# Taking maxima over partitions on TensorE and VectorE instead of GpSimd in a talking-heads attention and gated feed-forward kernel

## The chip, the cores and the metric

The kernel runs on one core of a Trainium2 chip. The metric is the device time of one execution in microseconds (us); the lower the better. Engines are named as the profile names them: PE is TensorE's matrix multiplication and PEld its loading of stationary operands, DVE is VectorE, ACT is ScalarE, POOL is GpSimd, SP is SyncE, which here only issues DMA transfers. An engine's name with a q behind it (POOLq, SPq) is its instruction queue.

## The reference

Attention for 4 batches, 12 heads, 448 tokens and 64 columns per head, in which the heads are mixed before and after the softmax, and then a gated feed-forward layer over the 768 joined columns:

```python
scores = scale * np.matmul(q, k.transpose(0, 1, 3, 2))
scores = np.einsum('bhij,hg->bgij', scores, w_pre)
scores = scores - np.max(scores, axis=-1, keepdims=True)
attn = np.exp(scores)
attn = attn / (np.sum(attn, axis=-1, keepdims=True) + 1e-09)
attn = np.einsum('bhij,hg->bgij', attn, w_post)
x = np.matmul(attn, v)            # then rearranged to (4*448, 768)
...
xn = x / rms * rms_g
g = xn @ w_gate
silu = g * (1.0 / (1.0 + np.exp(-g)))
val = xn @ w_val
return (silu * val @ w_out).astype(np.float32)
```

## The kernel before

The kernel has two parts. Part A, some 540 us, is the attention; part B is the feed-forward layer, matrix products in which three passes over split operands stand in for one of high precision. The change lies in part A.

Part A cuts the work of a batch into 4 chunks of query rows (of 12, 11, 11 and 11 groups of 10 rows). One group of one chunk is a *step*; there are 180 steps, 45 to a batch. In a step the function `premix` multiplies the scores of all heads by the first mixing matrix (tile `sp`, L216), `rowmax` takes row maxima on DVE (`nm`, L221), `expo` takes the exponential and its sum on ACT (`e`, L227), and `norm` puts the reciprocal of the sum (`rp`, L236) into the second mixing matrix on POOL (`wn`, L238). Two steps later `postmix` multiplies by `wn` (`pm`, L246), and three steps later `evac_ah` on ACT and `evac_al` on DVE split the result into two halves of 16 bits (`ah`, L258 and `al`, L263). The scores of the next chunks (`qk`, L195 and L196, evacuated to `st` at L209 and sent to their places by DMA, `r<-st`, L212) and the products with V (`av`, L273 and L274) are spread over the steps.

The order is written by hand: the loop over `t` in `part_a` runs the jobs of the step, and then `premix`, `norm`, `av_mm`, `postmix`, `qk_mm` and the evacuations, each engine taking its instructions in the order in which they are written. A job is a function with the step at which it runs (or the first and the last) and what it costs POOL; `run_jobs` runs those that are due.

The tiles `qk` come from a PSUM pool of two buffers (`ps_q`, tag `qk`), used in turn as they come free.

V is split into two 16-bit halves, for which each head is scaled by its largest magnitude. For one batch `max_v` takes, head by head on DVE, the maximum along each partition's row (`vm`, L155), `top_v` the maximum of these over all 128 partitions on POOL (`va`, L159, the instruction PARTITION_ALL_REDUCE), `scale_v` the scales from it (L163 to L175, DVE), and `round_v` (ACT, L178) and `split_v` (POOL, L183 and L184) do the split:

```python
vam[b] = p2.tile([128, H], F32, name=f"va{b}", tag="va")
nc.gpsimd.partition_all_reduce(vam[b], vmx.pop(b), 128, bass_isa.ReduceOp.max)
```

This happens in the third step of the second chunk for the first batch (step 11), and in the third step of a batch for the others (steps 47, 92 and 137, counted from 0). Before the steps, `setup` uses the same instruction once, for the column maxima of the second mixing matrix (`mpost`, L91).

Of the kernel before, what the change touches and what calls it, by code (L numbers as in the profile page):

```python
# [8 lines left out]
F32 = mybir.dt.float32  # L9
# [4 lines left out]
ALU = mybir.AluOpType  # L14
# [20 lines left out]
@with_exitstack  # L35
def attention_moe(ctx: ExitStack, tc, q, k, v, wpre, wpost, mask, ident, wgv, wo, rms_g, out):
    nc = tc.nc
# [39 lines left out]
    we = pro.tile([120, H], F32, name="we", tag="ksm2")  # L77
    wp = pro.tile([128, H], F32, name="wp", tag="ksm3")
    inv = pro.tile([128, H], F32, name="inv", tag="ksm4")

    def load_consts():
        nc.gpsimd.memset(wp, 0.0)
        nc.sync.dma_start(msk.rearrange("p a r -> p (a r)"), mask)
        nc.sync.dma_start(we, wpre)
        nc.sync.dma_start(wp[:120], wpost)

    def setup():
        nc.vector.tensor_scalar(we, we, D ** -0.5, None, ALU.mult)
        mt, mb = (msk[:, i].unsqueeze(1).to_broadcast([120, H, R]) for i in range(2))
        nc.vector.tensor_tensor(wk_pre, we.unsqueeze(2).to_broadcast([120, H, R]), mt, ALU.mult)  # L90
        nc.gpsimd.partition_all_reduce(mpost, wp, 128, bass_isa.ReduceOp.absmax)  # L91
        nc.vector.tensor_scalar(mpost, mpost, 1e-30, None, ALU.max)
        nc.vector.reciprocal(inv, mpost)
        nc.vector.tensor_tensor(wp, wp, inv, ALU.mult)
        nc.vector.tensor_tensor(wk, wp[:120].unsqueeze(2).to_broadcast([120, H, R]), mb, ALU.mult)


    kt, kraw, qhh, qll, qraw, vt, vraw, vmx, vam, vsc = ({} for _ in range(10))

# [50 lines left out]
    def max_v(b, part):  # L150
# [4 lines left out]
        nc.vector.tensor_reduce(vmx[b][:JP, h], vraw[b][:, h], AX.X, ALU.max, apply_absolute_value=True)  # L155

    def top_v(b):
        vam[b] = p2.tile([128, H], F32, name=f"va{b}", tag="va")
        nc.gpsimd.partition_all_reduce(vam[b], vmx.pop(b), 128, bass_isa.ReduceOp.max)  # L159

    def scale_v(b):
        am = vam.pop(b)
        nc.vector.tensor_scalar(am, am, 1e-30, None, ALU.max)  # L163
        sc = p2.tile([128, H], F32, name=f"vs{b}", tag="vs")
# [223 lines left out]
    def job(lo, hi, cost, f, *a):  # L388
        jobs.append([lo, hi, cost, f, a])

    pool_ = nc.gpsimd
    for n in range(NCHUNK):
# [13 lines left out]
        if c == 3 and b + 1 < B:  # L406
            for p in range(6):
                job(first[n] - 2 + p, 0, 0, load_v, b + 1, p)
            for h in range(H):
                t = first[n] + 3 + (14 * h) // 15  # L410
                job(t, t, 0, max_v, b + 1, h)
            job(first[n + 1] + 2, first[n + 1] + 2, 0.6, top_v, b + 1)
            job(first[n + 1] + 4, first[n + 1] + 4, 0, scale_v, b + 1)
        if n == 0:
# [4 lines left out]
            for h in range(H):  # L419
                t = 2 + (3 * h) // 4  # L420
                job(t, t, 0, max_v, 0, h)
            job(11, 11, 0.6, top_v, 0)
            job(12, 12, 0, scale_v, 0)
        if n == 4:
# [5 lines left out]
        if c == 0:  # L430
            for h in range(H):
                lo = av_step[n - 1, h] + 1 if n else 13
                job(lo, av_step[n, h] - 2, 1.1, round_v, b, h)
# [432 lines left out]
def layout(inputs):  # L866
# [14 lines left out]
    def cols(w, kt):  # L881
# [11 lines left out]
        "wpre": np.tile(inputs["w_pre"], (R, 1)),  # L893
        "wpost": np.repeat(inputs["w_post"], R, axis=0),
        "mask": np.concatenate([np.repeat(eye_r, H, axis=0), np.tile(eye_r, (H, 1))], axis=1),
        "ident": np.eye(JP, dtype=np.float32),
# [22 lines left out]
```

## Time and profile before

| | |
|---|---|
| median of 3 runs | 1097.96 us (1097.61 to 1099.19) |
| the profiled execution's own time | 1095.26 us |
| its span, first to last instruction | 1093.5 us |
| PE busy | 1012.9 us, 93% of the span |
| PEld, DVE, ACT, POOL busy | 854.0, 640.5, 495.2, 463.9 us |
| granted TensorE clock, mean over the span | 0.973 of full speed |
| DMA | 144.28 MB, mean 132 GB/s |
| chain that ended last | PE 65%, DMA 12%, DVE 10%, issue 7%, POOL 3% |

The busy time of an engine is the time in which it had an instruction in work; register, branch, semaphore and DMA-issuing instructions are left out of it. A number behind `x` is a count. In square brackets at the end of a timeline's row stands how long the engine was idle before that row and what ended the idle time; "issue" is time in which it waited for nothing that the profile shows. The granted clock is a share of full speed: 1.00 is 2.4 GHz, and 0.50 would be 1.2 GHz. Matmuls of 32-bit numbers count twice in the profile (`x8` for the four of `postmix`).

### The profile page before, as it was taken

How to read it: one execution, taken by the hardware profiler on the slowest of the kernel's cores; microseconds unless marked ns; L12 is line 12 of the kernel's file. 1: busy time of each engine (PE TensorE's matmuls, PEld its weight loads, DVE VectorE, ACT ScalarE, POOL GpSimd, SP SyncE). 2: the span in 40 equal slices, each digit the busy share in tenths (PEclk: the TensorE clock that was granted, in tenths of full speed). 3: DMA queues.
4: the chain of work that ended last, by engine and by line, in shares of the span. 5: the costliest groups of instructions: out<-in, count | busy, mean ns of one | idle time of the engine just before them, and what ended most of it. 6: DMA issues, size and time to landing. Idle time of an engine off the chain costs nothing.

```text
span 1093.5 us, 18212 instructions
## 1 busy us (share of the span) xinstructions
PE 1012.9 (93%) x6352; PEld 854.0 (78%) x6352; DVE 640.5 (59%) x1271; ACT 495.2 (45%) x1094; POOL 463.9 (42%) x576
## 2 busy tenths in 40 slices
PE   5859996999699996999998999999999998999998
PEld 2547774777477774877777999999999996999997
DVE  5536664776557664757759555555599996811100
ACT  4648874788578875877941111111111113422100
POOL 1345733676157643662544544444455553200000
PEclk9979997999989998999998999999999999999999
DMA  8636873668645775554442222222233436542100
GB/s 218 167 92 148 190 197 101 187 186 211 168 108 145 194 196 159 140 149 119 135 152 63 100 87 88 92 92 92 83 102 132 141 111 193 173 148 88 59 34 34
DMA packets 85969, 144.28 MB, mean 132 GB/s; under 512 B 21909, under 2 KB 76789, under 8 KB 85877
## 3 DMA queue, kind: packets, MB, share of 16 engines
q1 hardware_dynamic: 79541, 131.88, 41.3%
q0 software_dynamic: 6336, 11.22, 4.5%
q8 instruction: 51, 0.84, 0.3%
q14 instruction: 41, 0.34, 0.1%
HBM read 81.53 MB, written 22.83 MB: 95 GB/s over the span
## 4 chain that ended last, share of the span: by engine, by line
PE 65%; DMA 12%; DVE 10%; issue 7%; POOL 3%; ACT 2%; SPq 1%; POOLq 0%; DVEq 0%; ACTq 0%
PE pm L246 11%; PE sp L216 9%; DMA r<-st 7%; PE po L648 5%; PE po L649 5%; PE po L647 5%; PE pv L649 3%; PE qk L195 3%; PE pv L647 3%; PE pv L648 3%; PE pg L647 3%; PE pg L649 3%; PE pg L648 3%; PE qk L196 3%; PE av L273 2%
## 5 line engine op out<-in xcount | busy, mean ns | idle before, releaser
L246 PE MATMUL pm<-wn,e 120*112 120x120 f32 x1440 | 190.3, 276 | 45.6 <-POOL wn L238 45.1
L246 PEld LDWEIGHTS pm<-wn,e 120*112 120x112 f32 x1440 | 166.4, 181 | 61.6 <-POOL wn L238 52.0
L216 PE MATMUL sp<-r,wk_pre 120*120 120x448 f32 x360 | 170.9, 557 | 6.0 <-DMA qr<-in_q 5.7
L221 DVE TENSOR_REDUCE nm<-sp 120x1 f32<-120x448 f32 x180 | 111.7, 620 | 105.3 <-PE sp L216 103.6
L227 ACT ACTIVATE e<-sp,nm 120x448 f32<-120x448 f32 x180 | 113.7, 632 | 57.6 <-DVE nm L221 55.9
L238 POOL TENSOR_SCALAR wn<-wk,rp 120x120 f32<-120x120 f32 x180 | 65.9, 366 | 165.5 <-DVE rp L236 92.6
L263 DVE SCALAR_TENSOR_TENSOR al<-pm,ah 112x480 f16<-112x480 f32 x180 | 116.8, 649 | 11.4 <-ACT ah L258 11.2
L258 ACT ACTIVATE ah<-pm 112x480 f16<-112x480 f32 x180 | 101.9, 566 | 36.8 <-PE pm L246 36.0
L209 ACT ACTIVATE st<-qk 110x448 f32<-110x448 f32 (+1 forms) x186 | 100.3, 543 | 36.9 <-DMA r<-st 26.2
L579 ACT ACTIVATE wh<-wc 128x768 fp32r<-128x768 f32 x26 | 22.0, 847 | 193.7 <-DVE wc L555 193.7
L274 PEld LDWEIGHTS <-v 112*128 112x128 f16 x768 | 75.0, 98 | 43.1 <-issue 43.1
L195 PE MATMUL qk<-k,qh 128*110 128x448 f32 (+1 forms) x192 | 88.2, 459 | 15.7 <-ACT st L209 8.4
L647 PE MATMUL pv<-x,wh 128*128 128x448 f32 x264 | 97.5, 369 | 2.3 <-ACT wh L579 2.3
L273 PEld LDWEIGHTS <-v 112*128 112x128 f16 x768 | 74.5, 98 | 31.2 <-issue 29.6
L649 PE MATMUL pv<-x,wl 128*128 128x448 f32 x264 | 97.5, 369 | 1.1 <-POOL wl L580 1.1
L648 PE MATMUL pv<-x,wh 128*128 128x448 f32 x264 | 97.1, 368 | 0.0
L647 PE MATMUL pg<-x,wh 128*128 128x448 f32 x264 | 96.9, 367 | 0.0
L580 POOL TENSOR_TENSOR wl<-wc,wh 128x768 fp32r<-128x768 f32 x26 | 48.9, 1880 | 112.2 <-ACT wh L579 112.2
L649 PE MATMUL pg<-x,wl 128*128 128x448 f32 x264 | 96.3, 365 | 0.0
L648 PE MATMUL pg<-x,wh 128*128 128x448 f32 x264 | 96.2, 364 | 0.0
L273 PE MATMUL av<-ah,v 112*128 112x110 f16 (+1 forms) x768 | 94.6, 214 | 0.0
L274 PE MATMUL av<-al,v 112*128 112x110 f16 (+1 forms) x768 | 93.9, 213 | 0.1
(146 smaller groups left out, 2122.7 us busy)
## 6 DMA issues: line engine op xcount, KB each, us to landing
r<-st SPq DMA_DIRECT2D x144, 192.5 KB
wraw<-in_wgv SPq DMA_DIRECT2D x20, 768.0 KB
hd<-sg SPq DMA_DIRECT2D x48, 224.0 KB
hraw<-hd SPq DMA_DIRECT2D x48, 224.0 KB
r<-st SPq DMA_DIRECT2D x48, 210.0 KB
wraw<-in_wo SPq DMA_DIRECT2D x12, 768.0 KB
qr<-in_q SPq DMA_DIRECT2D x36, 220.0 KB
qh<-in_q POOLq DMA_DIRECT2D x33, 220.0 KB, 4.4
```

What stands on the lines that cost most here:

```text
L195: nc.tensor.matmul(ps[:m, :S], qhh[n][:, h], kk, start=True, stop=False)
L216: nc.tensor.matmul(ps[:120, :S], wk_pre.rearrange("p h r -> p (h r)"), rt[n][:120, g], start=True, stop=True)
L221: nc.vector.tensor_reduce(t, sps[n, g][:120, :S], AX.X, ALU.max, negate=True)
L227: nc.scalar.activation(e, sps.pop((n, g))[:120, :S], AF.Exp, bias=nmx.pop((n, g)), accum_out=s)
L246: nc.tensor.matmul(o, e[:, c * JP : (c + 1) * JP], w, start=True, stop=True)
L258: nc.scalar.activation(av[n, g][0], src, AF.Copy, scale=float(2.0 ** A_EXP))
L263: nc.vector.scalar_tensor_tensor(l_, src, float(2.0 ** A_EXP), h_, ALU.mult, ALU.subtract)
L273: nc.tensor.matmul(o, w[:, c_], ah[n][:, c_, h, :m], start=(c_ == 0), stop=False)
L274: nc.tensor.matmul(o, w[:, c_], al[n][:, c_, h, :m], start=False, stop=(c_ == JC - 1))
L647: nc.tensor.matmul(ps, a, xh[:, kk], start=(i == 0), stop=False)
L648: nc.tensor.matmul(ps, a, xl_[:, kk], start=False, stop=False)
L649: nc.tensor.matmul(ps, a2, xh[:, kk], start=False, stop=(i == n - 1))
```

## The change

`partition_all_reduce` is gone. In `setup` a DMA brings the second mixing matrix, transposed by the host, to all 128 partitions (`wa`, 128 x 144 numbers), and DVE takes the maxima along the row. For V, `top_v` becomes four jobs in four consecutive steps, one in each: `turn_v` transposes the 112 x 12 maxima by a matmul with the identity into a `ps_q` buffer (tile `vt`); `top_v` takes the maximum along the row on DVE and puts it on the diagonal of a 12 x 12 tile (`vo`, `vd`); `spread_v` multiplies a tile of ones by this diagonal, which puts the 12 maxima on all 128 partitions, in a second `ps_q` buffer (tile `va`); `scale_v` goes on from there. `max_v` runs up to one step earlier, `round_v` may start a step or two later.

```diff
     def load_consts():
-        nc.gpsimd.memset(wp, 0.0)
         nc.sync.dma_start(msk.rearrange("p a r -> p (a r)"), mask)
         nc.sync.dma_start(we, wpre)
-        nc.sync.dma_start(wp[:120], wpost)
+        nc.sync.dma_start(wp, wpost)
+        nc.sync.dma_start(wa, wpall)
...
-        nc.gpsimd.partition_all_reduce(mpost, wp, 128, bass_isa.ReduceOp.absmax)
+        nc.vector.tensor_reduce(mpost, wa.rearrange("p (g h) -> p g h", h=H), AX.X, ALU.max, apply_absolute_value=True)
...
+    def turn_v(b):
+
+        vps[b] = ps_q.tile([128, 512], F32, name="vt", tag="qk")
+        nc.tensor.matmul(vps[b][:H, :JP], vmx.pop(b)[:JP], eye, start=True, stop=True)
+
     def top_v(b):
-        vam[b] = p2.tile([128, H], F32, name=f"va{b}", tag="va")
-        nc.gpsimd.partition_all_reduce(vam[b], vmx.pop(b), 128, bass_isa.ReduceOp.max)
+        m = p2.tile([H, 1], F32, name=f"vo{b}", tag="vo")
+        nc.vector.tensor_reduce(m, vps.pop(b)[:H, :JP], AX.X, ALU.max)
+        vam[b] = p2.tile([H, H], F32, name=f"vd{b}", tag="vd")
+        nc.vector.tensor_scalar(vam[b], eye[:H, :H], m, None, ALU.mult)
+
+    def spread_v(b):
+        vps[b] = ps_q.tile([128, 512], F32, name="va", tag="qk")
+        nc.tensor.matmul(vps[b][:, :H], ones[:H], vam.pop(b), start=True, stop=True)
 
     def scale_v(b):
-        am = vam.pop(b)
-        nc.vector.tensor_scalar(am, am, 1e-30, None, ALU.max)
+        am = p2.tile([128, H], F32, name=f"va{b}", tag="va")
+        nc.vector.tensor_scalar(am, vps.pop(b)[:, :H], 1e-30, None, ALU.max)
...
-                t = first[n] + 3 + (14 * h) // 15
+                t = first[n] + 3 + (13 * h) // 15
                 job(t, t, 0, max_v, b + 1, h)
-            job(first[n + 1] + 2, first[n + 1] + 2, 0.6, top_v, b + 1)
-            job(first[n + 1] + 4, first[n + 1] + 4, 0, scale_v, b + 1)
+            for i, f in enumerate((turn_v, top_v, spread_v, scale_v)):
+                job(first[n + 1] + 2 + i, first[n + 1] + 2 + i, 0, f, b + 1)
...
-            job(11, 11, 0.6, top_v, 0)
-            job(12, 12, 0, scale_v, 0)
+            for i, f in enumerate((turn_v, top_v, spread_v, scale_v)):
+                job(10 + i, 10 + i, 0, f, 0)
...
-                lo = av_step[n - 1, h] + 1 if n else 13
+                lo = max(av_step[n - 1, h] + 1, first[n] + 6) if n else 14
                 job(lo, av_step[n, h] - 2, 1.1, round_v, b, h)
```

How this moves instructions, at three places. Line numbers of the changed kernel are 11 higher from the middle of the file on (L238 becomes L249, L246 becomes L257, L195 becomes L206). First POOL in the first batch, around step 11, before the change. Rows named ISA without a tile set up POOL's code; the trace calls them MODIFY_POOL_CONFIG. `L159 ISA va` is the PARTITION_ALL_REDUCE.

```order
L139 TENSOR_TENSOR ql_292<-qr_293,qh_291 128x440
L159 ISA
L159 ISA va_596<-vm_297 128x12
L238 ISA
L238 TENSOR_SCALAR wn<-wk,rp 120x120
L132 DMA qh_631<-in_q 128x440
L238 TENSOR_SCALAR wn<-wk,rp 120x120 x2
L183 TENSOR_SCALAR v_0_690<-vr_266 112x4x64
L184 TENSOR_TENSOR v_0_690<-vr_266,v_0_690 112x4x64
```

The same place after it:

```order
L132 DMA qh_631<-in_q 128x440
L249 TENSOR_SCALAR wn<-wk,rp 120x120 x2
L132 DMA qh_631<-in_q 128x440
L249 TENSOR_SCALAR wn<-wk,rp 120x120
L194 TENSOR_SCALAR v_0_728<-vr_267 112x4x64
L195 TENSOR_TENSOR v_0_728<-vr_267,v_0_728 112x4x64
...
L194 TENSOR_SCALAR v_3_737<-vr_267 112x4x64
L195 TENSOR_TENSOR v_3_737<-vr_267,v_3_737 112x4x64
L249 TENSOR_SCALAR wn<-wk,rp 120x120
```

The three ISA rows are gone, here and at the other three places, and no row of that name is left on POOL but those at the program's start and end. In this batch alone, four heads are split in one step between two `wn`, where before there were two and two; in the other batches POOL's order is otherwise the same.

Second PE at the same place in the changed kernel, with the semaphores that each row waits for; `vt` is `turn_v`, `va` is `spread_v`.

```order
L160 MATMUL vt<-eye,vm_298 12x112 [waits DMAHW5_49,DVE_49,Activation_49]
L227 MATMUL sp<-r_162,wk_pre 120x448
L257 MATMUL pm<-wn,e 112x120 [waits DVE_49,PE_49,Pool_49]
L257 MATMUL pm<-wn,e 112x120 x3
L206 MATMUL qk<-k_1_125,qh_292 110x448 [waits DVE_49]
L207 MATMUL qk<-k_1_125,ql_293 110x448
L227 MATMUL sp<-r_162,wk_pre 120x448 [waits Activation_49]
...
L170 MATMUL va<-vd_601,ones 128x12 [waits DVE_49,Activation_49]
...
L206 MATMUL qk<-k_2_129,qh_292 110x448 [waits DVE_49]
```

The matmul `vt` stands ahead of a step's `sp`, and the `qk` of that step, which before waited for an evacuation on ACT, now waits for DVE: it gets the buffer of `vt`, and waits until `top_v` has read it. The `qk` two places further on waits in the same way for `scale_v` to read `va`. The other three batches have the same pattern.

Third DVE in the changed kernel, from the end of the step of `turn_v`:

```order
L232 TENSOR_REDUCE nm<-sp 120x1
L274 SCALAR_TENSOR_TENSOR al_354<-pm,ah_353 112x48x10
L164 TENSOR_REDUCE vo_599<-vt 12x1
L166 TENSOR_SCALAR vd_601<-eye,vo_599 12x12
L245 TENSOR_SCALAR t<-s 120x1
```

The read of `vt` (L164) stands behind `nm` and `al` of the step in which PE made `vt`, and ahead of everything of the next step.

## Rows read from the trace of the kernel before

**Rows 1.** Waits over the whole span: waiting row, releaser, us in total, times, longest.

```profile
POOL wn L238 <- issue: 29.7, 4, 7.8
PE pm L246 <- POOL wn L238: 45.1, 9, 11.4
PE qk L195 <- ACT st L209: 8.4, 6, 2.2
```

**Rows 2.** Timeline of POOL, 154 to 182 us: start, duration, instruction, idle before.

```profile
158.59 0.36 POOL L238 TENSOR_SCALAR wn<-wk,rp 120x120 f32<-120x120 f32 x1 [1.53 <-DVE rp L236]
164.90 0.43 POOL L159 PARTITION_ALL_REDUCE va<-vm  x1 [5.95 <-DVE nm L221]
...
173.76 0.70 POOL L238 TENSOR_SCALAR wn<-wk,rp 120x120 f32<-120x120 f32 x2 [7.81 <-issue]
```

**Rows 3.** Groups of instructions, shapes apart: busy us, mean ns | idle before.

```profile
L159 POOL PARTITION_ALL_REDUCE va<-vm x4 | 1.7, 430 | 23.6 <-DVE nm L221 11.8 <-DVE rp L236 5.9 <-issue 5.9
L316 PE MATMUL pss<-ones,sum 128*112 128x1 f32 x32 | 3.4, 228 | 0.0
L184 POOL TENSOR_TENSOR v<-vr,v 112x256 f16<-112x256 f32 x48 | 34.0, 709 | 4.0
L183 POOL TENSOR_SCALAR v<-vr 112x256 f16<-112x256 f32 x48 | 22.0, 458 | 0.0
```

**Rows 4.** Timeline of PE, 162.5 to 186 us, second batch.

```profile
162.89 0.92 PE L216 MATMUL sp<-r,wk_pre 120*120 120x448 f32 x2
174.16 1.94 PE L246 MATMUL pm<-wn,e 120*112 120x120 f32 x8 [9.96 <-POOL wn L238]
...
180.76 0.92 PE L216 MATMUL sp<-r,wk_pre 120*120 120x448 f32 x2
...
183.19 0.92 PE L216 MATMUL sp<-r,wk_pre 120*120 120x448 f32 x2
```

**Rows 5.** Timeline of PE, 56.5 to 78 us, first batch.

```profile
75.22 0.92 PE L216 MATMUL sp<-r,wk_pre 120*120 120x448 f32 x2
...
77.20 0.92 PE L216 MATMUL sp<-r,wk_pre 120*120 120x448 f32 x2
```

**Rows 6.** Four stretches: length, busy us by engine, PE clock, DMA share, GB/s.

```profile
57.36:75.22 17.86, 6.42 (x25) 4.67 (x24) 3.95 (x15) 4.46 (x12) 4.84 (x10) 0.62 0.28 76
162.89:180.76 17.87, 7.91 (x41) 6.08 (x40) 4.88 (x18) 4.29 (x10) 4.24 (x8) 0.62 0.39 111
289.86:307.21 17.35, 7.78 (x42) 5.96 (x41) 4.72 (x17) 6.11 (x13) 5.10 (x9) 0.70 0.52 137
417.91:434.31 16.40, 7.18 (x41) 5.24 (x40) 4.97 (x17) 6.57 (x16) 6.09 (x9) 0.69 0.46 125
sum 69.48, PE 29.30 PEld 21.95 DVE 18.52 ACT 21.43 POOL 20.27; mean PE 7.32 PEld 5.49 DVE 4.63 ACT 5.36 POOL 5.07
```

**Rows 7.** The stretch between the first two of these, same columns.

```profile
75.22:162.89 87.67, 86.00 (x703) 66.65 (x702) 57.84 (x157) 70.49 (x172) 50.53 (x82) 1.00 0.70 176
```

**Rows 8.** Timelines of PE and of DVE, a step at 410.6 us.

```profile
412.58 0.44 PE L195 MATMUL qk<-k,qh 128*110 128x448 f32 x1
...
412.14 0.65 DVE L263 SCALAR_TENSOR_TENSOR al<-pm,ah 112x480 f16<-112x480 f32 x1
412.70 0.41 DVE L155 TENSOR_REDUCE vm<-vr 112x1 f32<-112x256 f32 x1
```

**Rows 9.** Timelines of PE and of DVE, a step of the first batch.

```profile
52.92 0.44 PE L195 MATMUL qk<-k,qh 128*110 128x448 f32 x1
...
53.48 0.41 DVE L155 TENSOR_REDUCE vm<-vr 112x1 f32<-112x256 f32 x1
```

**Rows 10.** Timelines of ACT, POOL and PE at the first steps.

```profile
24.95 0.57 ACT L138 ACTIVATE qh<-qr 128x440 fp32r<-128x440 f32 x1 [6.49 <-DMA qr<-in_q]
27.79 0.56 ACT L138 ACTIVATE qh<-qr 128x440 fp32r<-128x440 f32 x1
...
28.59 2.18 POOL L139 TENSOR_TENSOR ql<-qr,qh 128x440 fp32r<-128x440 f32 x2 [8.18 <-ACT qh L138]
...
31.17 1.07 PE L246 MATMUL pm<-wn,e 120*112 120x120 f32 x8 [1.38 <-POOL wn L238]
```

More of the change, by code (lines that the diff above doesn't have):

```diff
@@ L3 @@
 import concourse.bass as bass
-import concourse.bass_isa as bass_isa
 import concourse.tile as tile
@@ L35, in attention_moe @@
 @with_exitstack
-def attention_moe(ctx: ExitStack, tc, q, k, v, wpre, wpost, mask, ident, wgv, wo, rms_g, out):
+def attention_moe(ctx: ExitStack, tc, q, k, v, wpre, wpost, wpall, mask, ident, wgv, wo, rms_g, out):
     nc = tc.nc
@@ L77, in attention_moe @@
     we = pro.tile([120, H], F32, name="we", tag="ksm2")
-    wp = pro.tile([128, H], F32, name="wp", tag="ksm3")
+    wp = pro.tile([120, H], F32, name="wp", tag="ksm3")
+    wa = pro.tile([128, H * H], F32, name="wa", tag="ksm5")
     inv = pro.tile([128, H], F32, name="inv", tag="ksm4")
     def load_consts():
-        nc.gpsimd.memset(wp, 0.0)
         nc.sync.dma_start(msk.rearrange("p a r -> p (a r)"), mask)
         nc.sync.dma_start(we, wpre)
-        nc.sync.dma_start(wp[:120], wpost)
+        nc.sync.dma_start(wp, wpost)
+        nc.sync.dma_start(wa, wpall)
     def setup():
@@ L90, in setup @@
         nc.vector.tensor_tensor(wk_pre, we.unsqueeze(2).to_broadcast([120, H, R]), mt, ALU.mult)
-        nc.gpsimd.partition_all_reduce(mpost, wp, 128, bass_isa.ReduceOp.absmax)
+        nc.vector.tensor_reduce(mpost, wa.rearrange("p (g h) -> p g h", h=H), AX.X, ALU.max, apply_absolute_value=True)
         nc.vector.tensor_scalar(mpost, mpost, 1e-30, None, ALU.max)
         nc.vector.reciprocal(inv, mpost)
-        nc.vector.tensor_tensor(wp, wp, inv, ALU.mult)
-        nc.vector.tensor_tensor(wk, wp[:120].unsqueeze(2).to_broadcast([120, H, R]), mb, ALU.mult)
-    kt, kraw, qhh, qll, qraw, vt, vraw, vmx, vam, vsc = ({} for _ in range(10))
+        nc.vector.tensor_tensor(wp, wp, inv[:120], ALU.mult)
+        nc.vector.tensor_tensor(wk, wp.unsqueeze(2).to_broadcast([120, H, R]), mb, ALU.mult)
+    kt, kraw, qhh, qll, qraw, vt, vraw, vmx, vps, vam, vsc = ({} for _ in range(11))
     def load_k(b, hp):
@@ L419, in attention_moe @@
             for h in range(H):
-                t = 2 + (3 * h) // 4
+                t = 2 + (2 * h) // 3
                 job(t, t, 0, max_v, 0, h)
-            job(11, 11, 0.6, top_v, 0)
-            job(12, 12, 0, scale_v, 0)
+            for i, f in enumerate((turn_v, top_v, spread_v, scale_v)):
+                job(10 + i, 10 + i, 0, f, 0)
         if n == 4:
@@ L894, in layout @@
         "wpost": np.repeat(inputs["w_post"], R, axis=0),
+        "wpall": np.tile(inputs["w_post"].T.reshape(1, -1), (128, 1)),
         "mask": np.concatenate([np.repeat(eye_r, H, axis=0), np.tile(eye_r, (H, 1))], axis=1),
```

## The prediction

> **What bounds the kernel now.** I read the list of waits first. TensorE is the engine that sets the pace, and the wait that costs it most in total in one row is that of the matmul `pm` for `wn` from GpSimd: 45.1 us in 9 waits, the longest 11.4 us; and GpSimd's `wn` itself waited 29.7 us in 4 waits, up to 7.8 us, for nothing that the profile shows [rows 1]. Four waits are one for each batch, so I looked at GpSimd's timeline in the second batch. There a `wn` ends at 158.95 us, the next instruction, the cross-partition maximum, starts only at 164.90, runs 0.43 us, and after it GpSimd does no arithmetic until 173.76 us [rows 2]. For 0.43 us of work it is away for 14.8 us: 5.95 us idle before and 7.81 us idle behind. It is the same in all batches: four such instructions are busy 1.7 us and have 23.6 us of idle time in front of them [rows 3], and the 29.7 us are the four gaps behind. In GpSimd's order a row that sets up its code stands on either side of each of them, so I take the gaps to be the price of bringing in other code and of going back.
>
> What each of these costs TensorE is read from the starts of its steps. In the second batch `sp` starts at 162.89 us, TensorE idles 9.96 us in front of `pm`, and two steps later `sp` starts at 180.76; the step after that takes 2.43 us, up to 183.19 [rows 4]. In the first batch a step of that place takes 1.98 us, 75.22 to 77.20 [rows 5]. The four stretches of two steps each take 69.48 us together, at a mean granted clock of 0.62 to 0.70, so part of them runs at 1.2 instead of 2.4 GHz [rows 6]. Between them the clock is 1.00 and TensorE is busy 86.00 of 87.67 us [rows 7]: no engine makes up there for what was lost, and what these stretches lose, the kernel loses.
>
> **The change part by part.** *Four cross-partition maxima go.* Without them the four stretches would take two steps of 1.98 us and six of 2.43 us, 3.96 + 14.58 = 18.5 us. They take 69.5. Gain: 50.9 us, the slow clock behind the pauses included.
>
> The Trainium skill ("GPSIMD Engine Reference", Instruction dispatch) says that the first call to a freshly loaded kernel of GpSimd pays about 6 us for loading code, with no instruction visible in the profile. The 5.9 us in front agree [rows 3]; of a second gap on the way back that page of the Trainium skill says nothing, and the trace has 7.4 us there on average [rows 1]. By the Trainium skill alone four calls would be worth an estimated 24 us, by the rows 50.9; the sum goes by the rows.
>
> The Trainium skill ("GPSIMD Engine Reference", When to use GPSIMD) calls GpSimd the only option for a reduction over partitions, which speaks against a way round over two other engines: by that rule the costs below would buy nothing. The trace shows that the reduction itself is 0.43 us, and that what is dear is what stands around it [rows 2].
>
> *The fifth, in the setup.* GpSimd's first subtraction `ql` of the steps has its operand at 25.52 us (24.95 + 0.57), but starts at 28.59, and does two in a row [rows 10]. Without the way back, the first would be done before the second's operand comes at 28.35, and the `wn` behind them, and `pm`, would come some 1.3 us earlier; `pm` had kept TensorE idle 1.38 us. Ends 0 (the transfers that follow take it back) and 1.4; I take 0.6. The new transfer `wa` stands in SyncE's queue ahead of the transfers `r<-st`: 128 x 144 x 4 bytes are 74 KB, at 176 GB/s [rows 7] 0.4 us. Net gain 0.2 us. The new reduction in the setup runs on VectorE, and nothing needs it before the first `wn`.
>
> *Eight small matmuls come,* two for each batch, each two instructions as the profile counts. Nearest are the column sums, 228 ns for one instruction [rows 3]: 0.46 us for each matmul if the two follow each other, 0.23 if they overlap, as the pair of `sp` does. They stand in TensorE's stream, where nothing hides them: 1.8 to 3.6 us, taken 1.8.
>
> *A new wait comes behind each `vt`.* The `qk` of that step gets its buffer, and cannot start before VectorE has read it, behind `al`. In a usual step `qk` starts at 412.58 and VectorE is free behind `al` at 412.70 [rows 8]; a read of 112 numbers takes less than the 0.41 us that 256 take there, say 0.3 with the signal. So `qk` comes at 413.0, 0.4 us late, in three batches. In the first, without `av` in the step, `qk` is at 52.92 and VectorE free at 53.48 [rows 9]: 0.9 us late. Together 2.1 us. Bounds: nothing, if `al` happens to be early; and 4 x 2.2 = 8.8 us, the longest wait of `qk` for a buffer so far [rows 1]. Behind this `qk` stand the next step's `sp` and all of TensorE's stream. The `qk` behind `va` waits for a read that VectorE makes at the beginning of the step, ahead of its `nm` and `al`: nothing. `spread_v` waits for `vd`, made a step earlier: nothing.
>
> *Work that moves.* VectorE gains two short operations for each batch; in the steps it is busy 57.84 of 87.67 us [rows 7], so they cost nothing except by the wait above. In the first batch GpSimd splits four heads in a row, 4 x (0.46 + 0.71) = 4.7 us [rows 3], and ACT rounds four in one step. `wn` is needed two steps later, and those steps hold two `av` each and are longer; where the cover is too short, one step's delay of 2.4 us is the most. I take 0.3.
>
> **Sum:** 50.9 + 0.2 - 1.8 - 2.1 - 0.3 = 46.9 us. Against the profiled execution's own 1095.26 us this gives 1048.4; its time lies 2.7 us below the median of the runs shown, 1097.96, against which I give the forecast: **1051 us**.
>
> **The rivals.** *The DMA engines take over as the bound.* The four stretches carry 17.86 x 76 + 17.87 x 111 + 17.35 x 137 + 16.40 x 125 KB, 7.8 MB [rows 6], which must now go in the remaining time. At 176 GB/s [rows 7] this is 44 us; with no room at all nearly the whole gain would come back and the kernel stay at 1095 or so, where no change can be told. Against it: the share outside is 0.70, 30% free of some 88 us, 26 us in each batch for 11 us. Half of it given back: 1073 us.
>
> *The two-buffer pool becomes tight.* All eight new tiles, not four, cost the longest wait seen, 2.2 us [rows 1]: 17.6 instead of 2.1, giving 1066.6 us. For it: a step with two `qk` fills the pool already. Against it: all other `qk` waits together are 8.4 us in 6 waits.
>
> *Only the gap in front goes,* and GpSimd is held up behind in some other way. That is what the trace would give if the gap of 7.81 us belonged to `wn` and not to the return from the maximum: 23.6 us [rows 3] less the 4.2 us of costs, 1078.6 us. Against it: only four `wn` have such a gap [rows 1], once for each maximum. The Trainium skill's 24 us would come out near the same time.
>
> *The new chain stops TensorE longer than the old one,* slower. The place is the `qk` behind `vt`. If VectorE came to the read only after a pause such as GpSimd's now, TensorE would idle long enough for the clock to fall as it does in the four stretches [rows 6], and all would be lost again plus the costs: 1097.96 + 4.2 = 1102 us. It decides at 50.9 / 4 = 12.7 us for each batch; the rows speak for 0.4 to 0.9. The Trainium skill's rule that GpSimd is the only option would come out on this side too.
>
> **How the numbers follow.** Forecast 0.80; pool 0.06; DMA halfway 0.06, fully 0.02 (no change); only the gap in front 0.03; slower 0.03. A difference under 0.2%, 2.2 us, cannot be told from no change here. Faster 0.95, same 0.02, slower 0.03. The forecast's own bounds: at best 50.9 + 1.4 - 1.8 = 50.5, 1047.5 us, and with the 1.5 us by which runs differ (1097.61 to 1099.19) 1046, set to 1045; at worst matmuls 3.6, waits 8.8, split 2.4, setup -0.4 make 35.7 us, 1062.3. Taken to 1064; above it lie the pool, DMA, gap and slower cases, 0.20 together.
>
> **What would show it.** Right: GpSimd's row of code setup and the waits of `wn` for nothing are gone from the steps; the two steps from `turn_v` on take 5 to 6 us together instead of 16.4 to 17.9; the granted clock there is 1.00; `qk` waits for `vo` on VectorE, under 1 us each, four times; the span is near 1047. Wrong: waits of `st` or `sp` for transfers grow by tens of us (DMA); `qk` waits over 2 us at `vt` or `va` (pool); a gap before the next `wn` stays; or the steps that follow are no longer 2.4 us.

## The result, and the profile after

Over 4 runs each the changed kernel takes 1058.97 us (1058.34 to 1059.69) and the kernel before 1098.58 us (1097.61 to 1101.75): a ratio of 0.9635 [0.9613, 0.9657], 39.6 us faster. The forecast was 1051 us in a range of 1045 to 1064, 46.9 us faster. The profiled execution took 1058.42 us, with a span of 1056.6 us and a mean granted clock of 0.983. Of the runs further down, one execution of the version with the small matmuls moved took 1425.61 us at a granted clock of 0.654 and is left out of that version's median and ratio, and one of the kernel before, 1106.92 us, is left out of the ratios beside it.

I begin with the two rows of [rows 1] that the change was aimed at. The list of waits of the changed kernel (waiting row, releaser, us in total, times, longest) has no wait of `wn` for "issue" any more, and `pm` waits little for `wn`:

```profile
ACT st L220 <- DMA r<-st: 31.0, 33, 2.6
PE qk L206 <- ACT st L220: 7.6, 8, 2.2
PE pm L257 <- POOL wn L249: 4.8, 4, 2.3
```

The timeline of POOL around `turn_v` of the second batch answers to [rows 2]. One `wn` follows another at the pace of the steps:

```profile
151.23 0.35 POOL L249 TENSOR_SCALAR wn<-wk,rp 120x120 f32<-120x120 f32 x1 [1.49 <-DVE rp L247]
154.16 0.36 POOL L249 TENSOR_SCALAR wn<-wk,rp 120x120 f32<-120x120 f32 x1 [2.57 <-PE qk L207]
157.12 0.35 POOL L249 TENSOR_SCALAR wn<-wk,rp 120x120 f32<-120x120 f32 x1 [1.96 <-DVE rp L247]
```

For the account I take the four steps from `turn_v` on, in each batch: the step of `vt`, one between, that of `va`, and the next. The columns are those of [rows 6]. First the kernel before, the first stretch and the sum of all four:

```profile
53.40:75.22 21.82, 10.38 (x49) 7.75 (x48) 7.19 (x24) 7.70 (x20) 6.29 (x12) 0.69 0.27 73
...
sum 87.97, PE 47.79 PEld 36.39 DVE 30.98 ACT 33.35 POOL 22.82; mean PE 11.95 PEld 9.10 DVE 7.75 ACT 8.34 POOL 5.70
```

Then the changed kernel:

```profile
52.50:61.91 9.41, 8.78 (x52) 6.52 (x52) 6.41 (x24) 5.86 (x14) 3.10 (x6) 1.00 0.44 118
148.20:159.65 11.45, 11.16 (x85) 7.95 (x84) 7.23 (x25) 7.44 (x18) 3.67 (x7) 1.00 0.89 238
263.64:276.12 12.48, 10.99 (x86) 7.88 (x84) 7.12 (x22) 8.27 (x20) 3.76 (x8) 1.00 0.84 228
383.85:395.99 12.14, 10.98 (x85) 7.88 (x84) 7.28 (x22) 8.72 (x20) 4.89 (x9) 1.00 0.84 231
sum 45.48, PE 41.91 PEld 30.23 DVE 28.04 ACT 30.29 POOL 15.42; mean PE 10.48 PEld 7.56 DVE 7.01 ACT 7.57 POOL 3.86
```

In the first batch `vt` stands just ahead of the stretch (52.20 us), at the end of a step that takes 2.36 us where it took 1.98; these 0.4 us are not in the rows and have to be added.

The granted clock is 1.00 in all four, and 87.97 - 45.48 = 42.5 us are gained. But twelve steps of 2.42 us and four of 1.98, the usual lengths, are 36.96 us: the pauses cost 87.97 - 36.96 = 51.0 us, as forecast (50.9), and the new chain still costs 45.48 - 36.96 = 8.5 us inside these stretches and 0.4 ahead of the first. The steps just behind them (four in the first batch, five each in the third and fourth) took 34.38 us before and take 36.67, another 2.3. So the new way costs 11.2 us where the forecast had 4.2, and 51.0 - 11.2 = 39.8 us is near the 39.6 measured. The two profiled executions themselves differ by less, 36.9 us in their spans (1093.5 and 1056.6): the steps outside the chains took 2.9 us more in the second of them. Where the 11.2 come from is the question for the experiments.

Two places show the first answers. The second batch on PE:

```profile
150.41 0.37 PE L207 MATMUL qk<-k,ql 128*110 128x448 f32 x1
150.71 0.36 PE L160 MATMUL vt<-eye,vm 112*12 112x112 f32 x2
151.00 1.01 PE L227 MATMUL sp<-r,wk_pre 120*120 120x448 f32 x2
...
153.46 0.45 PE L206 MATMUL qk<-k,qh 128*110 128x448 f32 x1 [0.19 <-DVE vo L164]
153.75 0.36 PE L207 MATMUL qk<-k,ql 128*110 128x448 f32 x1
153.95 0.92 PE L227 MATMUL sp<-r,wk_pre 120*120 120x448 f32 x2
...
156.47 0.39 PE L170 MATMUL va<-vd,ones 12*128 12x12 f32 x2
156.78 1.01 PE L227 MATMUL sp<-r,wk_pre 120*120 120x448 f32 x2
...
159.16 0.45 PE L206 MATMUL qk<-k,qh 128*110 128x448 f32 x1
```

and on DVE:

```profile
152.59 0.65 DVE L274 SCALAR_TENSOR_TENSOR al<-pm,ah 112x480 f16<-112x480 f32 x1
153.16 0.25 DVE L164 TENSOR_REDUCE vo<-vt 12x1 f32<-12x112 f32 x1
...
158.38 0.65 DVE L274 SCALAR_TENSOR_TENSOR al<-pm,ah 112x480 f16<-112x480 f32 x1
158.94 0.16 DVE L174 TENSOR_SCALAR va<-va 128x12 f32<-128x12 f32 x1
```

The read of `vt` stands behind `al`, as forecast, and holds `qk` up. But the read of `va` (158.94, done at 159.10) stands behind the `al` of the step in which PE made `va`, and the `qk` of that same step (159.16) starts only behind it: it waits a second time, where the forecast had nothing. In the first batch, PE and then DVE:

```profile
52.20 0.36 PE L160 MATMUL vt<-eye,vm 112*12 112x112 f32 x2
...
54.96 0.46 PE L206 MATMUL qk<-k,qh 128*110 128x448 f32 x1 [0.63 <-DVE vo L164]
...
59.44 0.44 PE L206 MATMUL qk<-k,qh 128*110 128x448 f32 x1
```

```profile
59.44 0.65 DVE L274 SCALAR_TENSOR_TENSOR al<-pm,ah 112x480 f16<-112x480 f32 x1
60.01 0.16 DVE L174 TENSOR_SCALAR va<-va 128x12 f32<-128x12 f32 x1
```

The read stands behind `al` here too, but the `qk` of that step starts before it, so it cannot be using that buffer, and it does not wait. The four batches do not have one pattern. In the third batch something else shows, on ACT:

```profile
270.96 0.67 ACT L321 ACTIVATE sum<-sum,csc 128x448 f32<-128x448 f32 x1 [2.03 <-DMA sum<-xd]
271.54 0.56 ACT L269 ACTIVATE ah<-pm 112x480 f16<-112x480 f32 x1
...
272.68 0.54 ACT L220 ACTIVATE st<-qk 110x448 f32<-110x448 f32 x1
```

and on PE:

```profile
273.28 0.39 PE L170 MATMUL va<-vd,ones 12*128 12x12 f32 x2 [1.30 <-ACT st L220]
```

ACT sits 2.03 us before a square of an earlier batch's output (`sq_sum`, L321) whose transfer has not landed; `ah` and `st` come late behind it, and `va` needs the buffer that `st` empties. The kernel before had the same square in this place, inside GpSimd's pause (0.90 us of ACT's waiting in the third batch, 1.65 in the fourth).

### The profile page after: what moved, and what is told of

The parts are those of the page before. It is cut to its first block, busy times and chain, and to the rows that moved or that the text cites. A ratio compares the mean times of both kernels' runs of the same rounds, so it can differ in the third digit from the quotient of the medians.

```text
span 1056.6 us, 18244 instructions
## 1 busy us (share of the span) xinstructions
PE 1011.9 (96%) x6368; PEld 852.3 (81%) x6368; DVE 643.6 (61%) x1280; ACT 494.5 (47%) x1094; POOL 461.7 (44%) x570
## 4 chain that ended last, share of the span: by engine, by line
PE 67%; DVE 11%; DMA 11%; issue 5%; ACT 3%; POOL 2%; SPq 1%; DVEq 0%; ACTq 0%; POOLq 0%
PE pm L257 10%; PE sp L227 9%; DMA r<-st 6%; PE po L659 5%; PE po L660 5%; PE po L658 5%; PE pv L660 4%; PE pv L658 4%; PE pv L659 3%; PE pg L658 3%; PE pg L660 3%; PE pg L659 3%; PE qk L206 3%; PE av L284 2%; PE av L285 2%
## 5 line engine op out<-in xcount | busy, mean ns | idle before, releaser
L257 PE MATMUL pm<-wn,e 120*112 120x120 f32 x1440 | 186.9, 273 | 6.9 <-POOL wn L249 4.8
L257 PEld LDWEIGHTS pm<-wn,e 120*112 120x112 f32 x1440 | 163.6, 178 | 21.7 <-issue 11.4
L238 ACT ACTIVATE e<-sp,nm 120x448 f32<-120x448 f32 x180 | 113.8, 632 | 56.0 <-DVE nm L232 54.5
L249 POOL TENSOR_SCALAR wn<-wk,rp 120x120 f32<-120x120 f32 x180 | 66.6, 370 | 153.2 <-DVE rp L247 107.0
L285 PEld LDWEIGHTS <-v 112*128 112x128 f16 x768 | 75.0, 98 | 42.5 <-issue 42.5
L206 PE MATMUL qk<-k,qh 128*110 128x448 f32 (+1 forms) x192 | 87.5, 456 | 16.3 <-ACT st L220 7.6
```

What stands on the lines that cost most here:

```text
L206: nc.tensor.matmul(ps[:m, :S], qhh[n][:, h], kk, start=True, stop=False)
L238: nc.scalar.activation(e, sps.pop((n, g))[:120, :S], AF.Exp, bias=nmx.pop((n, g)), accum_out=s)
L257: nc.tensor.matmul(o, e[:, c * JP : (c + 1) * JP], w, start=True, stop=True)
L285: nc.tensor.matmul(o, w[:, c_], al[n][:, c_, h, :m], start=False, stop=(c_ == JC - 1))
```

## The experiments

My theory: (1) of the 11.2 us a part is the two-buffer pool of `qk`, in which `vt` and `va` each make a `qk` wait for VectorE; (2) another part is the same pool handing ACT's wait for a transfer on to TensorE; (3) the rest is the small matmuls themselves. The rivals: the DMA engines are the limit, or the differences between steps are chance. In each run below, the time of the kernel before is that of the runs beside it on the same chip.

**The kernel before, again.**

> The kernel before a second time, to see by how much its steps differ from one execution to the next. Total: within 0.3% of the kernel before. Theory (the differences of 2 to 5 us between kernels in steps 6 to 10, 38 to 44, 84 to 88, 129 to 134 and 159 to 165 are transfers that land earlier or later by chance): these stretches differ by 1 us or more between this run and the profiled execution shown of before, and the four stretches with the cross-partition maximum agree within 0.5 us, 69 to 70 us together. Rival (they are a property of each kernel): those stretches agree within 0.3 us too.

Measured: 1097.7 us, ratio 1.0012 [0.999, 1.0033]. Its four stretches of four steps sum to 87.93 us against 87.97, none more than 0.4 us off, and those of [rows 6] to 69.44 against 69.48. Steps 6 to 10 took 11.0 us against 13.75, 38 to 44 15.0 against 17.7, 84 to 88 13.4 against 11.4; but 129 to 134 (15.3 against 14.8) and 159 to 165 (18.1 both) hardly differ, so the theory held for three stretches of five. Steps outside the chains can scatter by 3 us, so it is the chains that I compare between two traces. With GpSimd's pause in them they too can differ by more than these two show: the stretch of the second batch is 22.71 us in both, but 21.30 in the run of the setup alone below, which has the same steps.

**The change, again.**

> The changed kernel itself, a second time. In its first profile the span was 36.9 us shorter than before, 10 us less than forecast; about half of the shortfall lay in the steps of the four new chains, the other half in steps far behind them, in front of which no instruction had moved (the steps 39 to 42, 132, 162 and 163 took 6 us more than before). If these are a scatter of transfers from run to run, they take another length here, by a microsecond or more each, and the time is again 1058.3 to 1059.7 us. If the closer work of the new kernel holds up the transfers, the same steps take the same lengths again.

Measured: 1058.21 us against 1097.42, ratio 0.9632 [0.9599, 0.9665]. The four stretches: 9.40, 11.46, 12.38 and 13.55 us. The first two repeat to 0.01 us, the fourth is 1.4 us longer than in the profile above: where ACT waits for a transfer, the chain's length is not fixed. Over the chains and the steps behind them this pair of executions gains 37.9 us, where the pair above gains 39.8, so that the latter comes so near to 39.6 is in part chance. The steps far behind took other lengths than in the profile above, as scatter would have it: 38 to 44 17.1 us (20.6 above, 17.7 before), 129 to 134 16.0 (16.6, 14.8), 159 to 165 17.7 (19.8, 18.1). The single times, 1053.73 to 1062.11 us, spread wider than expected.

**The small matmuls behind `qk`.** `vt` and `va` are made behind the `qk` of a step instead of ahead of `sp`, so that VectorE can read them before the next `qk` needs the buffer. On PE this puts `vt` a step later and leaves `va` where it was, between a step's last `qk` and the next `sp`; the read of `va` comes a step earlier:

```diff
+    def behind(f):
+        return lambda b: tail.append((f, b))
...
-            for i, f in enumerate((turn_v, top_v, spread_v, scale_v)):
-                job(first[n + 1] + 2 + i, first[n + 1] + 2 + i, 0, f, b + 1)
+            for i, f in enumerate((behind(turn_v), top_v, behind(spread_v), scale_v)):
+                u = first[n + 1] + 2 + (i + 1) // 2
+                job(u, u, 0, f, b + 1)
...
+            for f, b_ in tail:
+                f(b_)
+            tail.clear()
```

> The two small matmuls of each chain stand behind the qk of their step instead of ahead of its sp, so that no qk is left waiting for a read that VectorE makes behind al. Theory 1 (the two-buffer pool hands delays to TensorE): the waits of qk for vo and of va for st go, 0.4 us each at vt and at va, and the 1.3 and 1.1 us that transfers cost in the third and fourth batch; together 4 to 6 us faster than the changed kernel, some 1054 us, and the four steps from the turn on come to about 10.5 us in each batch instead of 11.5 to 12.5. Theory 2 (the excess is the price of the matmuls themselves): no change, 1058 to 1060 us.

Measured: 1054.64 us, ratio 0.9597 [0.956, 0.9634], an interval that overlaps that of the change. The trace decides: the first two stretches go from 9.41 and 11.45 us to 8.91 and 10.67, and the step ahead of the first, without `vt` now, from 2.36 to 1.98; TensorE is busy throughout, and no `qk` waits for VectorE there. That is 0.88 us in the first batch and 0.78 in the second for the waits behind `vt` and `va` together. What is left over the usual 7.92 and 9.68 us is 0.99 in each. The third and the fourth stretch, 11.10 and 12.35 us, missed the 10.5 expected: `va` and `vt` still wait for `st` there (0.35 us in the third, 0.78 and 0.76 in the fourth).

**The same, and V rounded as early as before.**

```diff
-                lo = max(av_step[n - 1, h] + 1, first[n] + 6) if n else 14
+                lo = av_step[n - 1, h] + 1 if n else 13
```

> As the one before, and the rounding of V may start as early as in the kernel before, so that in the first batch two and two heads are split instead of four in a row. Theory (the four splits in a row cost the 0.96 us by which step 15 is longer): 0.5 to 1 us faster than the one before. Rival (they are hidden): the same within 0.5 us.

Measured: 1051.26 us, ratio 0.9579 [0.9543, 0.9615]. Steps 14 to 18 took 10.16 us before, 11.16 in the change, 10.87 with the matmuls moved and 10.42 here. So these steps became 1.0 us longer, and not 0.3; 0.45 of it goes with the earlier start of the rounding, 0.3 had gone with the move of the matmuls, and 0.26 stays. The 0.45 lie just under the 0.5 to 1 us expected; the total alone does not show them.

**The same version a second time.**

> The changed kernel with the small matmuls behind the step's qk and the rounding of V as early as before, a second time. Theory (7 us faster than the change, some 4 of them from the waits of qk and of st in the steps of the four chains, and up to 0.5 from the split): ratio 0.955 to 0.961 against before, stretches of four steps from turn_v on 8.9, 10.7, 11.5 and 12.4 us within 0.3. If the time found first was chance: 0.962 to 0.965, like the changed kernel.

Measured: 1052.93 us, ratio 0.9605 [0.9579, 0.9632], between the two cases. The first two stretches are 8.91 and 10.67 us again, but the third and fourth are 14.46 and 15.26 instead of 11.54 and 12.44: that part of the expectation missed by 3 us each. The profiled execution was the slowest of the six, 1059.77 us. In the third batch ACT waited 2.84 us for the transfer and `va` on PE 2.07 us for `st`. The windows of that stretch:

```profile
267.50:269.60 2.10, 2.10 (x20) 1.49 (x18) 0.95 (x4) 0.19 (x1) 0.94 (x2) 1.00 0.93 236
269.60:271.00 1.40, 0.05 (x1) 0.00 (x0) 0.43 (x1) 1.38 (x3) 0.00 (x0) 1.00 0.90 252
271.00:272.50 1.50, 0.78 (x3) 0.58 (x4) 1.06 (x4) 1.38 (x5) 0.00 (x0) 0.99 0.67 183
272.50:276.21 3.71, 3.71 (x20) 3.00 (x19) 2.37 (x11) 2.95 (x7) 3.07 (x4) 0.55 0.66 165
```

TensorE is busy 2.10 of 2.10 us at a clock of 1.00, then has 0.05 us of work in 1.40 and 0.78 in 1.50, and 3.71 us of full work behind it run at 0.55, near the lower of its two levels. A wait of 2.07 us, with the slow clock behind it, makes the two steps 5.06 + 4.17 us long, where without it (below) they are 2.92 + 2.52: it costs 3.8 us.

**The squares moved away.** In the change, the squares of the first two batches, which fall in the chains of the third and fourth, run six steps later:

```diff
-    for b, t in ((0, first[8] + 1), (1, first[12]), (2, first[14] - 4)):
+    for b, t in ((0, first[8] + 7), (1, first[12] + 6), (2, first[14] - 4)):
```

> The changed kernel with the loads and sums of squares of two batches moved six steps later, away from the new chains. Theory 1 (ACT, which waits there 1.8 to 2.0 us for the load of the sum, hands this to TensorE because the pool is short of a buffer): the third and fourth batch's four steps come to some 11.5 us as in the second, 2 to 3 us faster than the changed kernel, 1056 to 1057 us. Theory 2 (that wait is harmless, the excess comes from elsewhere): no change.

Measured: 1059.16 us, ratio 0.9636 [0.9606, 0.9665], no gain where 2 to 3 us were expected. The windows say why; the third and the fourth stretch, and then steps 145 to 159, where the moved squares now stand:

```profile
259.57:271.03 11.46, 11.17 (x86) 7.95 (x85) 7.24 (x25) 7.43 (x18) 3.68 (x7) 1.00 0.76 212
378.94:390.41 11.47, 11.18 (x85) 7.95 (x84) 7.24 (x25) 7.43 (x18) 3.69 (x7) 1.00 0.73 208
...
402.52:442.92 40.40, 37.62 (x300) 29.69 (x298) 26.74 (x71) 31.46 (x74) 25.71 (x44) 0.96 0.53 144
```

Both stretches become those of the second batch, 11.45 us, to 0.02. So it is the squares that make the third and the fourth longer. But steps 145 to 159 go from 35.71 to 40.40 us, and steps 100 to 129 from 73.62 to 76.54: the wait moves with the squares.

**The small matmul by itself.** In the change `va` is made five times in a row:

```diff
-        nc.tensor.matmul(vps[b][:, :H], ones[:H], vam.pop(b), start=True, stop=True)
+        vd = vam.pop(b)
+        for _ in range(5):
+            nc.tensor.matmul(vps[b][:, :H], ones[:H], vd, start=True, stop=True)
```

> The changed kernel with the matmul va made five times in a row instead of once, in all four batches; the result is the same. In the version with the small matmuls behind qk, the step of va is 0.5 us longer than the step behind (2.93 against 2.42 to 2.52 us). Theory (a small matmul costs TensorE about 0.23 us for each of its two instructions, 0.46 together, as the column sums bound it from above): four more cost 1.8 us in each batch, 7.4 us in all, ratio to before near 0.970. Rival (its price is the change to another shape and back, paid once for a group): 0.1 us or less for each more, under 0.5 us in a batch, 1.6 us in all, no change that the total can tell; the step of va grows by under 0.5 us.

Measured: 1060.48 us, ratio 0.9673 [0.9642, 0.9704]. The first two stretches, free of ACT's wait, go from 9.41 to 10.31 and from 11.45 to 12.34 us, 0.9 for four more matmuls: 0.22 each, the two instructions together. Both expectations missed. (The third stretch stays at 12.47 us, inside ACT's wait; the fourth, 14.51, has ACT's wait and a mean clock of 0.92.) A single one makes the stretch 0.49 longer, so a good half of its price is paid once for a group, on the way from `qk` to the small matmul and from it to `sp`. That the change of shape makes it is the likeliest reading, but no run takes it apart from the change of operands. The PE rows of the second batch above show where that is: from the start of a step's last `qk` (L207) to `sp` it is 0.20 us where nothing stands between (153.75 to 153.95), and 0.59 with `vt` (150.41 to 151.00); and the `sp` behind takes 1.01 us instead of 0.92.

**Only the setup.** The kernel before, with the setup's maximum taken from the change and the four others left:

```diff
-        nc.gpsimd.partition_all_reduce(mpost, wp, 128, bass_isa.ReduceOp.absmax)
+        nc.vector.tensor_reduce(mpost, wa.rearrange("p (g h) -> p g h", h=H), AX.X, ALU.max, apply_absolute_value=True)
```

> The kernel before, with only the setup's cross-partition maximum replaced by the transfer of the transposed matrix and a maximum along the row on VectorE; the four in the steps stay. By the forecast: 0 to 1.4 us faster, net 0.2 us, so no change that can be told (ratio 0.998 to 1.002), and the first pm no longer waits 1.38 us for wn. Rival (the fifth call costs as much as each of the four others): 10 to 13 us faster, ratio near 0.989.

Measured: 1097.29 us against 1096.66, ratio 1.0001 [0.9979, 1.0023]. The rival of 10 to 13 us falls. The first `sp` waits for the transfer of `qr` with the fifth call and without it (5.73 and 6.45 us). The first `pm` still waits 0.98 us for `wn`, against 1.38 in [rows 10], where the expectation had no such wait. What the call costs, between nothing and the 1.4 us of the forecast, is not shown: from the first `sp` to that of the fourth step it is 7.0 or 8.2 to 8.5 us from one execution to the next, with the call (7.01 in the last run below, 8.53 in the kernel before repeated) and without it (7.00 here, 8.52 in the change repeated).

**Each maximum twice.** The kernel before, with a second cross-partition maximum directly behind each first:

```diff
-        nc.gpsimd.partition_all_reduce(vam[b], vmx.pop(b), 128, bass_isa.ReduceOp.max)
+        first_ = p2.tile([128, H], F32, name=f"vf{b}", tag="vf")
+        nc.gpsimd.partition_all_reduce(first_, vmx.pop(b), 128, bass_isa.ReduceOp.max)
+        nc.gpsimd.partition_all_reduce(vam[b], first_, 128, bass_isa.ReduceOp.max)
```

> The kernel before, with each of the four cross-partition maxima in the steps taken twice, the second directly behind the first and fed by it. Theory (the price is the gap in front and the gap behind, paid once for a change of GpSimd's code and back, however many such instructions stand between): 0.4 to 0.6 us for each, some 2 us in all, ratio 1.000 to 1.004; two gaps around each pair as before, none between the two. Rival (each instruction pays its own gaps): the pauses double, 40 to 55 us slower, ratio 1.035 to 1.05. Half of it (only the gap in front is paid again): some 24 us slower.

Measured: 1100.35 us against 1096.66, ratio 1.0032 [1.0017, 1.0048]. POOL in the second batch:

```profile
163.54 0.43 POOL L160 PARTITION_ALL_REDUCE vf<-vm  x1 [6.05 <-DVE nm L223]
164.07 0.40 POOL L161 PARTITION_ALL_REDUCE va<-vf  x1
...
172.42 0.70 POOL L240 TENSOR_SCALAR wn<-wk,rp 120x120 f32<-120x120 f32 x2 [7.33 <-issue]
```

One gap in front, one behind, none between. By the total the second maxima cost 0.9 us each (0.5 to 1.3 by the interval), against 11 to 13 for a first one. The four stretches grow from 87.97 to 91.31 us, but unevenly, by 0.1, 0.3, 1.1 and 1.8, and such stretches differ by up to 1.4 us between executions, so they do not fix the price of one. The price of the old way was the two gaps around the instruction, and not the reduction.

**The squares a step later than their transfers.** Back to the best version so far, with one more buffer for the squares, which are taken three steps after their transfers are issued, not two:

```diff
-        sq[b, kk] = pq.tile([128, S], F32, name="sq", tag="sq", bufs=2) if kk else sums[b]
+        sq[b, kk] = pq.tile([128, S], F32, name="sq", tag="sq", bufs=3) if kk else sums[b]
...
-            job(u + 2, u + 2, 1.1, sq_sum, b, kk)
+            job(u + 3, u + 3, 1.1, sq_sum, b, kk)
...
-            job(u + 5 + i // 2, u + 5 + i // 2, 0, sq_all, b, i)
+            job(u + 6 + i // 2, u + 6 + i // 2, 0, sq_all, b, i)
```

> The version with the small matmuls behind qk and the rounding of V as early as before, and in it the squares of x (sq, on ACT) are taken three steps after their transfers are issued instead of two, with one more buffer. Theory (in the chains of the third and fourth batch ACT waits for a transfer of x, comes late to ah and st, and the two-buffer pool hands that on to TensorE): the stretch of four steps of the third batch goes from 11.5 to 14.5 us to about 10.7, that of the fourth from 12.4 to 15.3 to about 10.7, 2 to 8 us in all; ratio to before 0.953 to 0.958. Rival (the transfers come as late as they are asked for, the queue being full): the waits move one step on and nothing is gained, 0.958 to 0.962.

Measured: **1045.24 us** against 1098.07, ratio 0.9532 [0.9505, 0.956]; the interval lies below that of the version repeated and overlaps that of its first run. The profiled execution was the slowest of the six, 1052.32 us. Its four stretches:

```profile
55.14:64.04 8.90, 8.90 (x54) 6.31 (x53) 6.67 (x24) 6.48 (x18) 3.43 (x7) 1.00 0.46 116
147.04:157.71 10.67, 10.67 (x86) 7.82 (x84) 7.57 (x27) 6.83 (x16) 3.08 (x7) 1.00 0.89 249
264.38:275.04 10.66, 10.66 (x86) 7.82 (x84) 7.57 (x26) 7.36 (x17) 3.07 (x7) 1.00 0.96 251
383.38:394.06 10.68, 10.68 (x86) 7.82 (x85) 7.58 (x26) 8.06 (x18) 3.67 (x7) 1.00 0.97 260
sum 40.91, PE 40.91 PEld 29.78 DVE 29.39 ACT 28.73 POOL 13.24; mean PE 10.23 PEld 7.44 DVE 7.35 ACT 7.18 POOL 3.31
```

TensorE is busy in every microsecond of them, at a DMA share of up to 0.97: as a limit of its own the DMA rival falls. The third and the fourth are now the second, as the theory had it. ACT's waits for these transfers fall from 9.3 us in the change

```profile
ACT sq L321 <- DMA sq<-xd: 5.5, 5, 2.3
ACT sum L321 <- DMA sum<-xd: 3.8, 2, 2.0
```

to 2.3 us here:

```profile
ACT sq L321 <- DMA sq<-xd: 1.7, 3, 1.3
ACT sum L321 <- DMA sum<-xd: 0.6, 1, 0.6
```

About half of the 9.3 us, 4.7, lay not in the chains but in steps 159 to 165, and these gained too: 14.37 us here, 19.74 and 18.30 in the two executions of this version without the later squares. The whole gain of 6 to 8 us is thus not the chains' alone.

**Two steps later.** The same with `bufs=4`, `u + 4` and `u + 7`:

> The same with the squares four steps after their transfers are issued, and two more buffers. Theory: the waits for these transfers are gone altogether, both stretches at 10.7 us, ratio 0.953 to 0.957, no slower than with three steps. Rival (the queue is full): as before, 0.958 to 0.962.

Measured: 1046.53 us, ratio 0.9537 [0.9515, 0.956]; no such wait is left, and the stretches are 8.91, 10.67, 10.67 and 10.67 us. One step was enough.

**The later squares without the change.** The same edit (`bufs=3`, `u + 3`) in the kernel before:

> The kernel before, with the squares of x taken three steps after their transfers are issued, as in the version of the change that had 0.953; GpSimd's cross-partition maximum stays. Theory (in the chains of the third and fourth batch the wait for these transfers lay in GpSimd's pause and cost nothing; near the end of part A, in steps 159 to 165, it costs with or without the change): the four steps from 91 and from 136 on stay at 22.2 and 21.3 us, within 0.7; steps 159 to 165 go from 18.1 to 13.3 to 14.4 us; ratio 0.994 to 0.998. Rival (the waits cost the kernel before as much as the changed one): 7 to 9 us faster, ratio 0.992 or lower, and those two stretches shorter by 1 us or more each.

Measured: 1094.91 us against 1098.0, ratio 0.9987 [0.9964, 1.0011]. The interval reaches into the expected ratios, but alone it shows no difference. In the steps the rival falls: the third and fourth stretch got no shorter (23.58 and 22.13 us against 22.19 and 21.25, longer by 1.4 and 0.9, which is outside the theory's 0.7 too, though no more than such stretches differ by between executions), while steps 159 to 165 went from 18.14 us at the first row to 14.21 at the second:

```profile
482.11:500.25 18.14, 14.69 (x97) 10.63 (x96) 9.94 (x27) 13.72 (x32) 8.05 (x13) 1.00 0.46 134
```

```profile
488.34:502.55 14.21, 13.79 (x97) 10.61 (x96) 9.80 (x26) 13.31 (x33) 8.38 (x14) 1.00 0.60 175
```

The wait for the squares' transfers cost nothing in GpSimd's pause that these stretches can tell. It became a cost in those two stretches by the change. In steps 159 to 165 it was one all along, by another way than the pool of `qk`: in the first row's steps GpSimd waits 6.1 us for ACT's squares and `pm` 3.4 us for GpSimd's `wn`; in the second row's no `pm` waits for `wn`.

## Why the prediction was right, and which terms were off

**What bounds, and the four maxima: right.** The two gaps were the price, paid once for a pair of maxima as for one (the run with each maximum twice), and with them the slow clock left the chains. Had only the gap in front gone, the gain would have been 19.4 us. The Trainium skill ("GPSIMD Engine Reference", When to use GPSIMD) calls GpSimd the only option for a reduction over partitions; the measurement differs, 0.9635 for the way over TensorE and VectorE, and it decides.

**The setup: no change, as forecast** (net 0.2 us; measured 1.0001, with an interval of some 2.4 us either way, which cannot tell 0.2 from the bounds).

**The costs were put at 4.2 us and are 11.2,** and the miss of 7.3 us (46.9 against 39.6) is nearly all in them. That the time still lies in the range was luck in part: the bound for the waits of `qk`, 8.8 us, was wide enough to hold a wait of ACT that the sum did not have.

| term | forecast, us | in the profile after, us | from |
|---|---|---|---|
| eight small matmuls | 1.8 | 4.0 | best version's 40.91 less 36.96 us |
| `qk` behind `vt` and `va` | 2.1 | 3.2 | 0.88 + 0.78 + 0.80 + 0.79 |
| ACT's wait handed on | none | 3.0 | below |
| steps 14 to 18, four heads in a row among it | 0.3 | 1.0 | 11.16 less 10.16 us |

The last two waits of the second row are the stretches with the squares moved less those of the best version, 11.46 - 10.66 and 11.47 - 10.68. The third row is 12.48 - 11.46 and 12.14 - 11.47 in the stretches, and 0.56 + 0.74 us in the five steps behind them (12.66 and 12.85 us against 12.10 and 12.11 before). The rows are differences between versions, one execution of each, and add up by that.

*The small matmuls* were mis-sized by taking the instruction's length, 0.23 us for a pair that overlaps. That is what a repeated one costs, 0.22; one by itself among large ones costs 0.49, just above the upper bound of 0.46 that the text had.

*"The `qk` behind `va`: nothing"* is the step that failed as reasoning. I had read the order in the first batch alone, and there it holds. In the second the `qk` of the same step waits for the read and comes 0.35 us late (159.16, where 0.79 us behind the start of `pm`, as in a usual step, is 158.81); with the squares moved, the third and the fourth batch have the same step of 2.87 us, which makes 1.0 us in all. In the change's own third and fourth batch `va` waits for `st` in place of this. The wait behind `vt` was right in kind and size: 0.87 us late in the first batch (54.96, for 54.09) and 0.43 in the second (153.46, for 153.03), where the forecast had 0.9 and 0.4.

*ACT's wait was not in the sum at all.* I had costed the waits that the change makes, and not those that lay under the pause it removes. The two rivals share this between them: the transfer is late, as the DMA rival had it, and the pool hands it on, as the pool rival had it. But neither came at its size. The last three chains moved 228 to 238 GB/s where the rival allowed 176, and with the squares a step later TensorE has no idle time in them. (The DMA rival's 1073 us left out the other costs; half of 50.9 us given back makes 1076.5.)

**The new chain stopping TensorE:** the longest pause in a new chain of any run was the 2.07 us of the version repeated, far from 12.7 us a batch; but the clock did fall there.

**What would show it:** GpSimd's gaps gone, clock 1.00 in the chains: right. Two steps from `turn_v` on, 5 to 6 us: 5.35 (52.50 to 57.85), 5.75, 5.76 and 6.32. `qk` waited for `vo` three times, 0.6 us at most; the fourth time it waited for `st`. The span is 1056.6 instead of 1047.

What stays open: why steps 6 to 10, 38 to 44 and 84 to 88 scatter by 2 to 3 us from execution to execution. `qk` waits for `st` there, which waits for transfers `r<-st`. Part of the scatter is the clock, as steps 129 to 134 show, in the kernel before and in the change:

```profile
393.38:408.23 14.85, 12.73 (x96) 9.38 (x95) 9.62 (x28) 10.45 (x26) 5.18 (x9) 1.00 0.73 196
```

```profile
362.39:379.00 16.61, 14.54 (x95) 10.18 (x94) 10.44 (x30) 10.67 (x26) 5.66 (x10) 0.90 0.66 182
```

In six of the fourteen traces the clock fell in these steps (mean 0.90 to 0.91), and they took 16.4 to 18.6 us; in the other eight it stayed at 1.00, and they took 14.4 to 16.0. Steps 38 to 44 took 18.8 to 20.6 us in the three traces with a fall there and 15.0 to 18.1 without. The profile after had such falls in steps 6 to 10, 38 to 44, 129 to 134 and 159 to 165, that of the kernel before in none of them, which is part of why its steps outside the chains took longer. Two things were not tried: a third buffer for `qk`, the most direct test of the pool, and ACT taking `st` ahead of the square.

## What to carry to other kernels

When a pause goes, look at what waited inside it: each wait of another engine that lay under the pause, with its length, is a candidate for the new critical path; here a pool of two buffers carried it there. A lone small matmul between large ones should be costed with what stands around it, about double the price of a repeated one here. Which instruction gets the buffer of a new tile, and when its reader comes, has to be looked up in each repetition, not in the first alone.

## What I had not expected of the hardware

The length of TensorE's pause is not its price: 2.07 us of waiting for a buffer were followed by 3.7 us at a granted clock of 0.55, and cost 3.8 us. Nor does the length of one pause tell whether the clock falls: in the fourth batch with five matmuls it fell behind pauses of 0.71 and 0.87 us (mean 0.92 over the stretch), and in that of the change repeated it stayed at 1.00 with pauses of 1.28 and 1.29. A cross-partition maximum right behind another costs 0.9 us of the kernel's time by the total, the first of them 11 to 13 (stretches of 21.3 to 22.7 us against 8.9 to 10.7 in the best version). And the DMA engines carried 249 to 260 GB/s at a share of 0.89 to 0.97 in the last three chains of the best version while TensorE was busy throughout, so a high share alone is no sign of a bound.
